# Building the routing's first twelve columns of comparisons during the last attention heads instead of after them

## The chip, the cores and the metric

One core of one Trainium2 chip runs the whole program. The metric is device time in microseconds (us), from start to end of one execution. The kernel is a single launch of three parts that follow each other: an attention, a mixture-of-experts layer whose routing depends on the attention's result, and a second feed-forward layer over the routed rows.

The engines are named as the profile names them. PE is TensorE (matmuls and transposes), DVE is VectorE, ACT is ScalarE, POOL is GpSimd, and SP is the queue that issues most transfers. Each engine works through its own list of instructions in the order in which the program wrote them.

## The reference

```
def _attn_ref(q, k, v, g_q, g_k):                  # 4 batches, 12 heads, 448 tokens, head dim 64
    q_n, k_n = (rmsnorm(q, g_q), rmsnorm(k, g_k))
    scores = scale * np.matmul(q_n, k_n.transpose(0, 1, 3, 2))
    scores = scores - np.max(scores, axis=-1, keepdims=True)
    attn = np.exp(scores)
    attn = attn / (np.sum(attn, axis=-1, keepdims=True) + 1e-09)
    return np.matmul(attn, v)

def _moe_ref(x, w_gate, w1, w2):                   # 1792 tokens, width 768, 8 experts, hidden 1024
    cap = N // E                                   # 224 tokens for each expert
    logits = x @ w_gate
    order = np.argsort(-logits.flatten())          # all token-expert pairs, best first
    for idx in order:                              # a token goes to its best expert that has room
        tok, e = (int(idx) // E, int(idx) % E)
        if assigned[tok] >= 0 or counts[e] >= cap:
            continue
        assigned[tok] = e
        counts[e] += 1
    for e in range(E):
        h = np.maximum(x[assigned == e] @ w1[e], 0.0)
        out[assigned == e] = h @ w2[e]
    return out

def _moe2_ref(x, w_in, w_out):                     # hidden 2048
    h = x @ w_in
    g = h * (1.0 / (1.0 + np.exp(-1.702 * h)))
    return g @ w_out
```

All tensors are float32. The order in which pairs are taken decides which tokens an expert gets, so the kernel has to rank tokens by their logits exactly.

## The kernel before

**Attention.** 48 heads follow each other (4 batches of 12, numbered 0 to 47). The list `ORDER` writes out, for each head, the order in which pieces of work are put on the engines' lists. The names that matter here: K0 and K1 are the score matmuls of the two halves of the head (tile `S`, two buffers), M0 and M1 the row maxima on DVE (line 233), E0 and E1 the exponentials on ACT, A0 to A3 the transposes on PE (tile `pA`, two buffers) of the head before, C0 to C3 the copies of those transposes (on ACT or DVE by `COPY_ENGINE`; block 1 is always on DVE), TQ and TK the transposes of the next head's queries and keys, LK the low part of the keys on DVE (`klo`, line 214), AV the product with the values. At odd heads XT transposes a finished pair of heads back to tokens and XP scales it on DVE (`xt`, line 305). GA and GB give the gate's logits of a batch. S4 and S5 are places where other work is let in, by a call of `slot(h, 4)` or `slot(h, 5)`. TQ, TK, XT, GA, GB and the routing's rows all use one PSUM buffer, the tile `tp`; who writes it next waits until its last reader is done.

**Conversion.** `Convert` turns the second layer's weights from 64-bit words into floats, 48 pieces of two steps each: 512 KB in, two ACT operations (`wab`, `wc`), two DVE operations (`wc`, lines 900 and 905), 256 KB out. One step is let in at S4 of every head up to 45; the rest runs beside the first experts, paced by a budget in `Moe.back`.

**Routing.** The tokens lie as 16 columns of 112; batch b fills columns 4b to 4b+3. `choose` finds each token's best expert and logit (six short DVE operations, lines 538 to 543). `row` spreads the logits of four columns over all partitions (four transposes into `tp`, one ACT copy into `vr`). `compare(j, t0, t1)` builds, on DVE, the 0/1 tile of the tokens of columns t0 to t1 against column j (lines 772 and 774: strictly less up to column j, less or equal behind it). `rank` gathers four such tiles and multiplies them with `Cp` on PE, so that PSUM counts for each token how many better ones each expert has. `same(j)` adds the tie mask of the diagonal on POOL (lines 759 and 760). `last_columns` does `choose`, `row` and `rest` for columns 12 to 15 once the last batch's logits are there; `rest` builds the tiles of columns 13, 14 and 15 on ACT by a Sign and a Relu of 112x1344 each (lines 554 and 555), and four diagonals on POOL. `close` then picks the expert that fills first and the ids of its tokens, and only then the first expert's weights and rows can be fetched.

`Route.first` is a generator: each `next(early)` runs it to its next `yield`. Before the change it is called at S5 of heads 44 to 47 (`choose` for columns 0 to 11, then the three rows), twice between the transposes of head 47, and the rest in `beside` after the attention. The counts go into the four banks of `S`, which are free only once the last exponentials of head 47 have read their scores; the tiles go into buffers of the attention that are free by then (`A`, `AT`).

In `Attn.run` the three calls at the end read

```
        beside(BESIDE[0])
        s.gate_b(s.B - 1, 1)
        beside(0)
...
        beside(BESIDE[1])
```

and `beside(0)` stands for `last_columns`.

Of the kernel before, what the change touches and what calls it, by code (L numbers as in the profile page):

```python
# [20 lines left out]
FT = mybir.dt.float32  # L21
FR = mybir.dt.float32r
F16 = mybir.dt.float16
# [3 lines left out]
OP = mybir.AluOpType  # L27
# [2 lines left out]


SLOT_CONVERT = ((4,), (4,))
BESIDE = [3, 5, [(48, 1), (48, 3)]]
LO_VECTOR = [(0, 2, 4, 6, 8, 10, 12), (1, 3, 5, 7, 8, 11, 13)]
IDLE = (2, 4, 5)
GATE_A = (0, 4)
# [15 lines left out]
class Attn:  # L52
# [294 lines left out]
    def wide(s):  # L347
        return s.ps.tile([128, 4, 112], FT, name="tp", bufs=1)[:112]
# [15 lines left out]
    def buffer2(s):  # L364
        t = s.io.tile([112, 4, 256], FT, name="qt", bufs=3).rearrange("p a b -> p (a b)")
        return t.bitcast(F16)[:, 0:1344].rearrange("p (j t) -> p j t", t=112)

    def small(s):
        return s.ps.tile([128, 4, 112], FT, name="pA", bufs=2)


    def run(s, slot, beside):
# [86 lines left out]
        s.gate_a(s.B - 1, 1)  # L459
# [3 lines that stand above are left out]
        for pr in (last - 2, last - 1, last):  # L463
            s.xtok(pr, True)
            s.put_x(pr, True)
        beside(BESIDE[1])


class Route:
# [241 lines left out]
    def phase(s, k):  # L711
# [28 lines left out]
        if k in (1, 3):  # L740
            yield from s.together(n, n - 4, small)

    def first(s, rank, wide, small, buffer, buffer2):

        nc, V, wk = s.nc, s.nc.vector, s.wk
        s.tiles()
        s.choose(0, 12)
        yield
        for c in range(3):
            s.row(c, wide())  # L750
            yield
        bank = rank()

        ready, diag = {}, {}

        def same(j):
            e = wk.tile([112, 112], FT, name="Be", bufs=1)
            d = wk.tile([112, 112], F16, name="Bd", bufs=16)
            nc.gpsimd.tensor_scalar(e, s.vr[:, j], s.v[:, j:j + 1], None, op0=OP.is_equal)
            nc.gpsimd.tensor_tensor(d, e, s.before, op=OP.mult)  # L760
            diag[j] = d

        def compare(j, t0, t1):
            sv = s.v[:, j:j + 1]
            b = ready.pop((j, t0), None)
            onact = b is not None
            if not onact:
                b = buffer(t0)
            d = diag[j] if t0 <= j < t1 else None
            k = min(max(j + 1, t0), t1)  # L770
            if t0 < k and not onact:
                V.tensor_scalar(b[:, 0:k - t0], s.vr[:, t0:k], sv, None, op0=OP.is_lt)
            if k < t1:
                V.tensor_scalar(b[:, k - t0:t1 - t0], s.vr[:, k:t1], sv, None, op0=OP.is_le)

            s.rank(j, b, d, bank, t0, t1, j < 4, j >= 12)

        def rest():
            for i in ON_ACT[0]:
                b = buffer2()  # L780
                s.lower(b[:, 0:12], s.vr[:, 0:12], s.v[:, i:i + 1])
                ready[i, 0] = b
            for i in range(12, 16):
                same(i)

        s.rest = rest
        for j in range(12):
            if j == 0:
                for i in range(12):
                    same(i)  # L790
            compare(j, 0, 12)
            yield
        for j in range(12, 16):
            if j not in ON_ACT[0]:
                compare(j, 0, 12)
        for j in range(12):
            compare(j, 12, 16)
        for j in ON_ACT[0]:
            compare(j, 0, 12)
        s.flush()  # L800
        yield
        for c in range(3):
            nc.scalar.copy(s.ct[:, 4 * c:4 * c + 4], bank[c])
        for j in range(12, 16):
            compare(j, 12, 16)
        s.flush()
        cnt = wide()
        s.counts(0, 12, cnt)
        nc.scalar.copy(s.ct[:, 12:16], bank[3])
        s.counts(12, 16, cnt)  # L810
        for _ in s.close(0, 16, small):
            pass
# [428 lines left out]
def kernel(  # L1241
# [31 lines left out]
    with ExitStack() as actx:  # L1273
        attn = Attn(actx, tc, q, k, v, g_q, g_k, w_gate, dict(identf=identf, identr=identr), xd, rec[:, :, 0:8])
        attn.ident128 = ident128
        route = Route(tc, consts, wk, rec, identf, ident128, dram)
        early = route.first(attn.rank_banks, attn.wide, attn.small, attn.buffer, attn.buffer2)

        def slot(h, at):
            if 0 <= h < 46:  # L1280
                for _ in range(SLOT_CONVERT[h % 2].count(at)):
                    conv.step()
            if at == 5 and h in (44, 45, 46, 47) or (h, at) in BESIDE[2]:
                next(early)

        def beside(n):
            if n:
                for _ in range(n):
                    next(early)
            else:  # L1290
                route.last_columns(attn.wide)

        attn.run(slot, beside)
        for _ in early:
            pass
# [35 lines left out]
```

## Time and profile before

| what | value |
|---|---|
| median of 3 runs | 1256.66 us (1256.13 to 1257.18) |
| the profiled execution | 1258.07 us, of which the span from first to last instruction is 1256.2 us |
| PE busy | 1147.1 us (91% of the span) |
| DVE busy | 854.4 us (68%) |
| ACT busy | 659.2 us (52%) |
| POOL busy | 703.8 us (56%) |
| granted PE clock, mean | 0.952 of full speed |

The busy shares are means over stages that differ. The stretch that the change touches lies between 293 us (head 43) and 365 us (the first expert's rows are gathered), 6% of the span. A chain of waits lists, in order of time, the pieces of work that each had to wait for the one ahead. The times of the tables below count from the start of the span.

### The profile page before, as it was taken

How to read it: one execution, taken by the hardware profiler on the slowest of the kernel's cores; microseconds unless marked ns; L12 is line 12 of the kernel's file. 1: busy time of each engine (PE TensorE's matmuls, PEld its weight loads, DVE VectorE, ACT ScalarE, POOL GpSimd, SP SyncE). 2: the span in 40 equal slices, each digit the busy share in tenths (PEclk: the TensorE clock that was granted, in tenths of full speed). 3: DMA queues.
4: the chain of work that ended last, by engine and by line, in shares of the span. 5: the costliest groups of instructions: out<-in, count | busy, mean ns of one | idle time of the engine just before them, and what ended most of it. 6: DMA issues, size and time to landing. Idle time of an engine off the chain costs nothing.

```text
span 1256.2 us, 19391 instructions
## 1 busy us (share of the span) xinstructions
PE 1147.1 (91%) x6952; PEld 965.6 (77%) x6952; DVE 854.4 (68%) x1525; ACT 659.2 (52%) x1289; POOL 703.8 (56%) x591
## 2 busy tenths in 40 slices
PE   4899999999858978789999999999999899999995
PEld 3677677766436867679889898998889799889995
DVE  7799999998779879687677836538864535751100
ACT  4798898888622356653335554224544323545420
POOL 3688688873634546455634765546454455445552
PEclk9799999999958889889999999999999899999998
DMA  6454555432043399944346634337633245753421
GB/s 164 118 136 130 150 130 141 127 97 67 24 120 109 98 265 277 276 149 160 117 130 174 183 115 116 121 98 208 192 110 117 93 120 151 199 166 113 135 78 33
DMA packets 185504, 172.95 MB, mean 138 GB/s; under 512 B 9536, under 2 KB 159808, under 8 KB 185408
## 3 DMA queue, kind: packets, MB, share of 16 engines
q1 hardware_dynamic: 180080, 160.55, 45.3%
q0 software_dynamic: 4224, 11.14, 2.9%
q8 instruction: 55, 0.90, 0.3%
q14 instruction: 41, 0.34, 0.1%
q10 hardware_dynamic: 1104, 0.03, 0.0%
HBM read 147.96 MB, written 23.72 MB: 137 GB/s over the span
## 4 chain that ended last, share of the span: by engine, by line
PE 67%; DVE 19%; DMA 5%; issue 5%; ACT 2%; POOL 1%; SPq 0%; POOLq 0%; DVEq 0%; ACTq 0%
PE mm L1029 12%; PE mm L1031 12%; PE mm L1030 12%; PE S L222 6%; PE mm L1040 5%; PE av L269 5%; PE pA L249 5%; PE mm L1041 3%; DMA dout<-wc 2%; DVE gs L1086 2%; DVE wc L900 2%; DVE B L571 2%; DVE tt L1082 2%; DMA xg<-xd,idx 1%; DVE B L569 1%
## 5 line engine op out<-in xcount | busy, mean ns | idle before, releaser
L968 POOL TENSOR_TENSOR wlo<-raw,whi 128x768 fp32r<-128x768 f32 (+1 forms) x175 | 382.3, 2187 | 384.0 <-ACT whi L965 361.3
L965 ACT CAST whi<-raw 128x768 fp32r<-128x768 f32 (+1 forms) x224 | 207.0, 924 | 151.5 <-issue 61.5
L1029 PE MATMUL mm<-gs,whi 128*128 128x448 f32 (+1 forms) x432 | 159.6, 369 | 0.5 <-DVE zs L1079 0.5
L1031 PE MATMUL mm<-gs,wlo 128*128 128x448 f32 (+1 forms) x432 | 156.2, 361 | 0.0
L1030 PE MATMUL mm<-gs,whi 128*128 128x448 f32 (+1 forms) x432 | 156.1, 361 | 0.0
L1031 PE MATMUL mm<-zs,wlo 128*128 128x448 f32 x384 | 143.3, 373 | 7.1 <-POOL wlo L968 4.0
L1029 PE MATMUL mm<-zs,whi 128*128 128x448 f32 x384 | 144.8, 377 | 3.1 <-ACT whi L965 3.1
L1030 PE MATMUL mm<-zs,whi 128*128 128x448 f32 x384 | 142.7, 372 | 1.4 <-DVE zs L1088 1.4
L240 ACT ACTIVATE A<-S,sm 112x448 f32<-112x448 f32 x192 | 122.6, 658 | 6.5 <-DVE sm L233 6.5
L1040 PE MATMUL mm<-gs,whi 128*128 128x448 f32 x336 | 111.6, 387 | 14.6 <-DVE gs L1086 12.7
L233 DVE TENSOR_REDUCE sm<-S 112x2 f32<-112x896 f32 x96 | 104.1, 1085 | 21.3 <-PE S L222 20.1
L1040 PE MATMUL mm<-xs,whi 128*128 128x448 f32 x336 | 111.6, 389 | 0.5 <-ACT whi L965 0.4
L249 PE MATMUL pA<-ident,A 112*112 112x112 f32 x768 | 100.9, 266 | 2.6 <-DVE AT L258 2.4
L1101 DVE TENSOR_TENSOR gs<-sg,gs 128x448 fp32r<-128x448 f32 x64 | 42.2, 662 | 82.5 <-ACT gs L1100 82.4
L249 PEld LDWEIGHTS pA<-ident,A 112*112 112x112 f32 x768 | 85.1, 137 | 14.9 <-DVE AT L258 3.6
L1029 PEld LDWEIGHTS mm<-gs,whi 128*128 128x128 f32 x432 | 83.6, 193 | 10.6 <-issue 4.3
L1099 ACT ACTIVATE sg<-mm 128x448 f32<-128x448 f32 x64 | 34.9, 545 | 104.6 <-PE mm L1031 104.6
L1031 PEld LDWEIGHTS mm<-gs,wlo 128*128 128x128 f32 x432 | 83.5, 193 | 6.1
L1030 PEld LDWEIGHTS mm<-gs,whi 128*128 128x128 f32 x432 | 83.7, 194 | 5.7
L1041 PE MATMUL mm<-xs,wlo 128*128 128x224 f32 x336 | 83.1, 275 | 3.6 <-POOL spacer L1138 1.9
L1031 PEld LDWEIGHTS mm<-zs,wlo 128*128 128x128 f32 x384 | 73.8, 192 | 15.1 <-POOL wlo L968 5.2
L1041 PE MATMUL mm<-gs,wlo 128*128 128x224 f32 x336 | 84.3, 272 | 1.0 <-DVE wlo L968 1.0
(229 smaller groups left out, 2626.1 us busy)
## 6 DMA issues: line engine op xcount, KB each, us to landing
raw<-in_moe_w_dram SPq DMA_DIRECT2D x64, 384.0 KB, 3.5
raw<-in_moe_w_dram SPq DMA_DIRECT2D x48, 512.0 KB, 5.1
raw<-din SPq DMA_DIRECT2D x64, 384.0 KB, 3.1
raw<-dout SPq DMA_DIRECT2D x48, 512.0 KB, 3.7
r<-in_moe_w_in_dram SPq DMA_DIRECT2D x24, 512.0 KB, 4.4
r<-in_moe_w_out_dram SPq DMA_DIRECT2D x24, 512.0 KB, 5.0
din<-wc SPq DMA_DIRECT2D x24, 256.0 KB, 4.2
dout<-wc SPq DMA_DIRECT2D x48, 128.0 KB, 4.9
```

What stands on the lines that cost most here:

```text
L222: nc.tensor.matmul(p[:, c, 0:448], s.qT[h][:, i, :], mv.rearrange("p i t -> p (i t)"), start=(n == 0), stop=(n == 1))
L233: s.nc.vector.tensor_reduce(s.sums[h][:, 2 * u:2 * u + 2, 0], s.Sp[u][:, :, 0:448], axis=AX.X, op=OP.max, negate=True)
L240: s.nc.scalar.activation(s.A[h][:, i, :], p[:, c, 0:448], AF.Exp, bias=sm[:, i, 0:1], scale=1.0, accum_out=sm[:, i, 1:2])
L249: nc.tensor.transpose(p[:, qc], s.A[h][:, qc, kc * 112:(kc + 1) * 112], s.identf)
L269: nc.tensor.matmul(p[hh * 64:(hh + 1) * 64, :], s.grp[g]["v"][:, hl, kc * 64:(kc + 1) * 64], s.AT[h][:, kc, :], start=(kc == 0), stop=(kc ...
L965: nc.scalar.copy(hi, t)
L968: f = lambda: eng.tensor_tensor(lo, t, hi.bitcast(FT), op=OP.subtract)
L1029: nc.tensor.matmul(p, hi[:, k], x[0], start=first, stop=False)
L1030: nc.tensor.matmul(p, hi[:, k], x[1], start=False, stop=False)
L1031: nc.tensor.matmul(p, lo[:, k], x[0], start=False, stop=last)
L1040: a = lambda: nc.tensor.matmul(p, hi[:, k], x.rearrange("p h t -> p (h t)"), start=first, stop=last)
L1041: b = lambda: nc.tensor.matmul(p[:, 0:224], lo[:, k], x[:, 0], start=False, stop=False)
```

## The change

The routing of columns 0 to 11 starts earlier and is cut in two. `choose` is called at S5 of head 42, the three rows at S4 and S5 of head 43 and at S4 of head 44. From S5 of head 44 on, twelve new steps build the twelve comparison tiles of columns 0 to 11 on DVE and keep them in `ready`, in buffers that a new function `buffer3` takes (`kt`, `qt`, `qp`, `kd`, `sq`, `sk`). The banks of `S` are asked for afterwards, at the end of head 47, and three further steps put the counting matmuls of these tiles on PE, four columns at a time. A table `EARLY` says at which place how many steps are run. The conversion's steps at heads 44 and 45 are dropped from there, so that these two steps are run later.

```
-BESIDE = [3, 5, [(48, 1), (48, 3)]]
+BESIDE = [1, 0]
+EARLY = [(42, 5), (43, 4), (43, 5), (44, 4), (44, 5), (45, 4), (45, 4), (45, 5), (46, 4), (46, 4), (46, 5),
+         (47, 4), (47, 4), (47, 5), (48, 0), (48, 0), (48, 1), (48, 3)]
...
+    def buffer3(s, j):
+
+        k = (j - 1) % 3
+        if j == 0:
+            s.room = s.io.tile([112, 4, 256], FT, name="kt", bufs=3).rearrange("p a b -> p (a b)")
+        elif j < 4:
+            s.room = s.io.tile([112, 4, 256], FT, name="qt", bufs=3).rearrange("p a b -> p (a b)")
+        elif j < 10:
...
+            s.room = s.wide_room[:, k * 672:k * 672 + 672]
+        else:
+            s.room = s.wk.tile([112, 16, 64], FT, name="sq" if j == 10 else "sk", bufs=1).rearrange("p a b -> p (a b)")
+        return s.room[:, 0:672].bitcast(F16).rearrange("p (j t) -> p j t", t=112)
...
         for c in range(3):
             s.row(c, wide())
             yield
-        bank = rank()
-
...
-            if k < t1:
+            if k < t1 and not onact:
                 V.tensor_scalar(b[:, k - t0:t1 - t0], s.vr[:, k:t1], sv, None, op0=OP.is_le)
...
         for j in range(12):
+            b, sv = buffer3(j), s.v[:, j:j + 1]
+            V.tensor_scalar(b[:, 0:j + 1], s.vr[:, 0:j + 1], sv, None, op0=OP.is_lt)
+            if j < 11:
+                V.tensor_scalar(b[:, j + 1:12], s.vr[:, j + 1:12], sv, None, op0=OP.is_le)
+            ready[j, 0] = b
             if j == 0:
                 for i in range(12):
                     same(i)
+            yield
+        for j in range(12):
+            if j == 0:
+                bank = rank()
             compare(j, 0, 12)
-            yield
+            if j % 4 == 3:
+                s.flush()
+                yield
...
         def slot(h, at):
-            if 0 <= h < 46:
+            if 0 <= h < 44:
                 for _ in range(SLOT_CONVERT[h % 2].count(at)):
                     conv.step()
-            if at == 5 and h in (44, 45, 46, 47) or (h, at) in BESIDE[2]:
+            for _ in range(EARLY.count((h, at))):
                 next(early)
```

`BESIDE[1]` is now 0, and the three calls at the end of `Attn.run` are as they were, so the last of them calls `last_columns` a second time.

Where the instructions stand, on PE first: the rows of the routing among the transposes into `tp` (`v` is a column's logits, `xu` a finished pair of heads). Before, at the end of head 45:

```order
L269 MATMUL av<-AT,vt 64x448 x4
L293 MATMUL tp<-ident_62,xu 112x128 x4
L549 MATMUL tp<-ident_62,v 112x112 x4
L222 MATMUL S<-khi,qT 112x448
L222 MATMUL S<-klo,qT 112x448
```

With the change, at the end of head 43:

```order
L271 MATMUL av<-AT,vt 64x448 x4
L568 MATMUL tp<-ident_62,v 112x112 x4
L295 MATMUL tp<-ident_62,xu 112x128 x4
L568 MATMUL tp<-ident_62,v 112x112 x4
L224 MATMUL S<-khi,qT 112x448
L224 MATMUL S<-klo,qT 112x448
```

Two rows now stand around the pair's transposes, ahead of the next head's scores, where one stood; the third row moves from the end of head 47 to head 44.

On ACT, the end of the attention (`vr` is the row of columns 12 to 15, `qt` a Sign or Relu of `rest`, `kt` the last three pairs of heads, `ct` the finished counts). Before:

```order
L550 COPY vr<-tp 112x448
L554 ACTIVATE qt<-vr,v 112x1344
L555 ACTIVATE qt<-qt 112x1344
L554 ACTIVATE qt<-vr,v 112x1344
L555 ACTIVATE qt<-qt 112x1344
L554 ACTIVATE qt<-vr,v 112x1344
L555 ACTIVATE qt<-qt 112x1344
L301 COPY kt<-pA 112x512 x2
L301 COPY kt<-av 112x512
L803 CAST ct<-S 128x448 x3
```

With the change, from the third Relu on:

```order
L574 ACTIVATE qt<-qt 112x1344
L303 COPY kt<-pA 112x512 x2
L303 COPY kt<-av 112x512
L569 COPY vr<-tp 112x448
L573 ACTIVATE qt<-vr,v 112x1344
L574 ACTIVATE qt<-qt 112x1344
L573 ACTIVATE qt<-vr,v 112x1344
L574 ACTIVATE qt<-qt 112x1344
L573 ACTIVATE qt<-vr,v 112x1344
L574 ACTIVATE qt<-qt 112x1344
L831 CAST ct<-S 128x448 x3
```

The row's copy and its six activations stand on ACT's list twice, the second time between the pairs' copies and the counts.

On DVE, the end of the attention, from the last batch's logits (`rec`) on, with the change:

```order
L341 TENSOR_REDUCE rec_68<-prod 112x4x8
L557 TENSOR_REDUCE v<-rec_68 112x4
L558 TENSOR_TENSOR ra_3849<-rec_68,v 112x32
...
L562 TENSOR_TENSOR Cp<-ra_3849,alive 112x4x8
L557 TENSOR_REDUCE v<-rec_68 112x4
...
L562 TENSOR_TENSOR Cp<-ra_3849,alive 112x4x8
L789 TENSOR_SCALAR A<-vr,v 112x1344
L791 TENSOR_SCALAR vt<-vr,v 112x448 x12
```

`choose` stands there twice, and behind it one comparison of columns 0 to 11 (column 12) where there were fifteen instructions for columns 5 to 12; the twelve `vt` are the comparisons with the tokens of columns 12 to 15.

## Rows read from the trace of the kernel before

**Rows 1.** Chain of waits, end of the attention: start (us), length, work and count.

```profile
334.50 0.45 PE tp L329 x4
...
353.90 1.41 ACT ct L803 x3
```

**Rows 2.** Heads 45, 46, 47, the counting: length, busy time by engine, PE clock, DMA.

```profile
305.00:312.70 7.70, 6.92 (x51) 4.85 (x49) 6.87 (x16) 6.37 (x17) 0.00 (x0) 1.00 0.14 42
312.70:318.75 6.05, 6.05 (x48) 4.42 (x45) 4.21 (x7) 5.10 (x15) 3.98 (x8) 1.00 0.46 125
318.75:325.90 7.15, 7.15 (x47) 4.21 (x45) 3.48 (x6) 5.01 (x14) 4.71 (x10) 1.00 0.01 2
...
338.30:354.00 15.70, 10.38 (x73) 3.22 (x73) 15.70 (x32) 8.78 (x10) 10.81 (x11) 0.71 0.18 45
```

**Rows 3.** Chain of waits at heads 43 and 45: start (us), length, work and count.

```profile
294.17 0.88 DVE rec L339
295.06 1.00 DVE sm L233
...
296.64 0.59 PE pA L249 x4
...
298.89 0.58 PE tp L293 x4
...
311.56 0.70 DVE xt L305
312.31 0.59 PE tp L549 x4
```

**Rows 4.** Timeline of ACT: start (us), length, work, and idle time before it.

```profile
299.55 0.68 ACT L886 ACTIVATE wab<-r 128x512 f32<-128x512 f32 x1
300.11 0.69 ACT L887 ACTIVATE wc<-r 128x512 int32<-128x512 uint32 x1
...
337.09 0.54 ACT L550 COPY vr<-tp 112x448 f32<-112x448 f32 x1 [2.65 <-PE tp L549]
...
342.87 1.40 ACT L554 ACTIVATE qt<-vr,v 112x1344 f16<-112x1344 f32 x1
...
345.53 1.05 ACT L301 COPY kt<-pA 112x512 f32<-112x512 f32 x2
346.47 0.60 ACT L301 COPY kt<-av 112x512 f32<-112x512 f32 x1
```

**Rows 5.** Timeline of DVE: start (us), length, work.

```profile
305.45 0.20 DVE L538 TENSOR_REDUCE v<-rec 112x12 f32<-112x96 f32 x1
...
307.03 1.08 DVE L233 TENSOR_REDUCE sm<-S 112x2 f32<-112x896 f32 x1
...
345.56 6.97 DVE L774 TENSOR_SCALAR vt<-vr,v 112x448 f16<-112x448 f32 x12
...
353.93 0.44 DVE L772 TENSOR_SCALAR vt<-vr,v 112x448 f16<-112x448 f32 x1
```

**Rows 6.** Busy time of the comparisons of columns 0 to 11, line 772, then line 774.

```profile
327.40:344.60 17.20, 7.30 (x12) 1.00 0.00 1
...
327.40:345.50 18.10, 6.88 (x11) 0.98 0.00 1
```

**Rows 7.** Counting matmuls of four columns: durations (ns, least, median, most), first and last start.

```profile
L592 PE MATMUL S<-A,Cp x12: 352/353/363, 338.3 to 338.7; 112*32 112x448 f16 x12
```

**Rows 8.** Stretches around one PE gap (columns as Rows 2).

```profile
503.00:505.00 2.00, 0.38 (x2) 0.36 (x3) 0.33 (x1) 1.44 (x3) 1.84 (x3) 1.00 0.98 233
505.00:507.00 2.00, 2.00 (x8) 1.76 (x7) 1.59 (x3) 0.68 (x1) 1.18 (x1) 0.56 1.05 375
507.00:509.00 2.00, 2.00 (x8) 1.79 (x7) 0.66 (x1) 1.36 (x3) 0.00 (x0) 0.58 1.06 369
```

**Rows 9.** The stretch of the conversion's last eleven pieces (columns as Rows 2).

```profile
497.00:541.00 44.00, 33.75 (x141) 28.40 (x140) 30.60 (x54) 27.63 (x47) 19.25 (x12) 0.87 0.92 277
```

**Rows 10.** The conversion's first ACT operation there: durations, first and last start.

```profile
L886 ACT ACTIVATE wab<-r x11: 658/672/703, 496.9 to 531.9; 128x512 f32<-128x512 f32 x11
```

More of the change, by code (lines that the diff above doesn't have):

```diff
@@ L366, in buffer2 @@
         return t.bitcast(F16)[:, 0:1344].rearrange("p (j t) -> p j t", t=112)
+    def buffer3(s, j):
[5 more added lines that the diff above has]
+        elif j < 10:
+            if k == 0:
+                s.wide_room = (s.wk.tile([112, 16, 128], FR, name="qp").bitcast(FT) if j < 7 else
+                               s.wk.tile([112, 16, 2, 64], FT, name="kd").rearrange("p a b c -> p a (b c)"))
+                s.wide_room = s.wide_room.rearrange("p a b -> p (a b)")
+            s.room = s.wide_room[:, k * 672:k * 672 + 672]
+        else:
+            s.room = s.wk.tile([112, 16, 64], FT, name="sq" if j == 10 else "sk", bufs=1).rearrange("p a b -> p (a b)")
+        return s.room[:, 0:672].bitcast(F16).rearrange("p (j t) -> p j t", t=112)
     def small(s):
@@ L741, in phase, with first @@
             yield from s.together(n, n - 4, small)
-    def first(s, rank, wide, small, buffer, buffer2):
+    def first(s, rank, wide, small, buffer, buffer2, buffer3):
         nc, V, wk = s.nc, s.nc.vector, s.wk
@@ L1276 @@
         route = Route(tc, consts, wk, rec, identf, ident128, dram)
-        early = route.first(attn.rank_banks, attn.wide, attn.small, attn.buffer, attn.buffer2)
+        early = route.first(attn.rank_banks, attn.wide, attn.small, attn.buffer, attn.buffer2, attn.buffer3)
         def slot(h, at):
-            if 0 <= h < 46:
+            if 0 <= h < 44:
                 for _ in range(SLOT_CONVERT[h % 2].count(at)):
                     conv.step()
-            if at == 5 and h in (44, 45, 46, 47) or (h, at) in BESIDE[2]:
+            for _ in range(EARLY.count((h, at))):
                 next(early)
```

## The prediction, made before the changed kernel ran

> **What bounds the kernel now.** I read the chain of waits first, then stretches of the timeline head by head. In the heads the chain runs almost wholly on PE, which is busy for all of heads 46 and 47 and for all but 0.8 us of head 45 [rows 2]. The reader should see in the same rows how much of each head VectorE is idle: 0.8, 1.8 and 3.7 us. At the end of head 42 the chain leaves PE: the reduction of the logits, the row maximum of head 43, a copy, and only then the transposes that PE waits for [rows 3]. After the heads it leaves PE again. While the comparisons are counted VectorE is busy for 15.70 of 15.70 us and PE waits for it [rows 2], from the gate's last transposes at 334.50 to the first copy of finished counts at 353.90 [rows 1]. So comparisons on VectorE cost time after the heads, and the heads seem to have room. What the room costs is decided by what else stands in the queues.
>
> **The change part by part.**
>
> *`choose` at the end of head 42.* Its six operations take 1.58 us, from 305.45 to the maximum behind them at 307.03 [rows 5]. They now stand between `rec` and the maximum of head 43, two pieces that follow each other on the chain without a gap, and the transposes at 296.64 wait on what comes behind [rows 3]. All but a tenth lies on the path: +1.5 us. Its old place at head 44 is not on the chain, so nothing comes back. Bounds: 0.5 (PE catches up) to 1.6.
>
> *Rows 0 and 1 at head 43.* Both stand on PE ahead of the scores of head 44, around the pair's transposes, and all three write the one buffer `tp`. Row 0 is copied by ACT, and on ACT's list the two conversion operations of this head's step stand ahead of that copy. They begin at 299.55 and 300.11 and end near 300.7 [rows 4]; with the 1.5 us of `choose` in front, near 302.3. The copy takes 0.5, so the pair's transposes start near 302.8 where they started at 298.89 [rows 3], 3.9 later. Then row 1 waits for the pair's scaling, 0.70 as at 311.56, and itself takes 0.59 [rows 3]. In all the scores of head 44 come 5.3 us late, 3.8 more than `choose` alone makes. Queued behind the waiting transposes is all of PE's work. Bounds: 2.5 (if ACT's exponentials are less late than VectorE) to 4.2.
>
> *Row 2 at head 44.* Only its own 0.4 us on PE.
>
> *The comparisons, heads 44 to 47.* Twelve tiles in 23 instructions have 7.30 + 6.88 = 14.2 us of busy time [rows 6]. Instructions of one engine overlap by 0.08 us in the timeline, so they occupy VectorE for 12.3, or 1.03 a tile. One fits into head 44. For heads 45 to 47 VectorE's list was 6.87 + 4.21 + 3.48 = 14.6 us [rows 2]. It loses `choose` (1.6) and one conversion step (0.6) and gains eleven tiles (11.3): 23.7 us. It also starts a microsecond after the head's first scores. PE's list over these heads was 20.9 us [rows 2], and without the rows and their wait it is near 19. So VectorE is late by head 47, and late then are the copies of the transposes of heads 46 and 47, which hold `pA`. Against before, the last of these transposes come 1 to 2 us later.
>
> *Counting on PE.* Three groups of 12 matmuls and 4 diagonals now stand among the last gate's steps. Twelve start within 0.4 us [rows 7], so a group takes about 0.65, and the first two are in front of the gate's last step. With the point above: lower bound +0.5 (VectorE not late, 1.5 us of row wait at head 45 saved, 2.0 us of groups added), upper +3.0 (the queue of 23.7 us in full). I take +2.3, nearer the upper end, since 23.7 is far above 19.
>
> Up to the row of the last columns that makes 1.5 + 3.8 + 0.4 + 2.3 = **+8.0 us**.
>
> *PE's clock.* At head 43 PE waits some 2.1 us before the pair's transposes and a further 1 us before row 1. The nearest row is the stretch at 503, where PE worked 0.38 of 2 us. There the clock stood at 0.56 and 0.58 of full for the next 4 us [rows 8], mostly the 1.2 GHz level, which cost 4 x 0.43 = 1.7 us. The wait of 0.8 us at head 45 cost nothing: the clock there is 1.00 [rows 2]. I take **+1.7**, with 0 as the lower end. The Trainium skill, "TensorE: Matmul & The Clock Gate", Part 1, says that an idle TensorE is throttled to half its rate and gets the full rate back only after it has been busy again. The trace agrees at 505, and the rule speaks against any wait put on PE. By it alone head 47's wait would cost the same again, 1.7 more.
>
> *`last_columns` twice.* `beside(BESIDE[1])` is now `beside(0)`. The second `choose` overwrites `v`, which the first pass's three Signs on ACT and four diagonals on GpSimd still read, so VectorE stops until the third Sign is done. Behind it are the comparison of column 12 and, after the second row, the twelve `vt`. Count from the start T of the first row's copy, before at 337.09 [rows 4]. The third Sign ended at 344.27, T + 7.2. ACT goes on with its Relu to T + 8.4 (345.53), then the three copies, 1.5 us, to T + 10.0 [rows 4]. Only then comes the second row's copy, and another 8.4 us to the last Relu at T + 18.4. VectorE's `vt`, 6.97 us [rows 5], end at T + 17.5 and are hidden. From the last `vt` (345.56 + 6.97 = 352.53) to the first copy of counts (353.90) were 1.4 us [rows 1, 5]. Counts are therefore copied at T + 19.8, where before it was 353.90 - 337.09 = 16.8: **+3.0 us**. Without the second pass the `vt` would end near T + 8.4 (0.5 for the row, 0.9 for column 12, 6.97), and the counts would be copied at T + 10.0, behind ACT's three copies, which is 6.8 us better than before. That is the most that the change can give here, and the second pass takes it all.
>
> *The conversion.* One piece moves from heads 44 and 45 to the end of the conversion, where eleven pieces [rows 10] go with 44.0 - 33.75 = 10.25 us of idle PE [rows 9]: **+0.9 us** a piece. Bounds: 0, and 4 (a whole 44/11 us of it). The ACT and VectorE time that it leaves in the heads is counted above.
>
> **Sum.** 8.0 + 1.7 + 3.0 + 0.9 = +13.6 us, on the profiled execution's 1258.07: 1271.7. The median of the runs is 1.4 below that execution, so against it I predict **1270.3 us**.
>
> **The rivals.**
> 1. *The clock holds at head 43.* For it: head 45's wait left it at 1.00. Against it: the wait is now more than twice as long. 1270.3 - 1.7 = 1268.6.
> 2. *The heads absorb the early work.* For it: VectorE's idle time above. Against it: the `tp` chain is on PE and ACT, where VectorE's room doesn't help. Up to the row +0.5 instead of 8.0, clock full: 0.5 + 3.0 + 0.9 = +4.4, 1261.1.
> 3. *Faster: the second pass hides.* Place: VectorE's list after the row. Price: -6.8 instead of +3.0. It decides if ACT's second pass ends before VectorE's comparisons and the delay up to the row, clock included, stays under 3.4 us. With that at 0.5: -6.8 + 0.5 + 0.9 = -5.4, 1251.3. Against it: the second row's copy is behind the three copies on ACT by the program's own order.
> 4. *GpSimd slows the comparisons.* GpSimd now makes its twelve diagonals beside the tiles of heads 45 and 46. In the `vt`, of which a part ran beside GpSimd, one took 6.97/12 = 0.58 us, where a like comparison alone took 0.44 less the overlap of 0.08 [rows 5]; at that ratio six tiles (6.2 us) would cost at most 3.8 more, and as most of this is in the mean of 1.03 already, I count +2.5: 1272.8. The Trainium skill, "GPSIMD Engine Reference", Key points, says that GpSimd shares its SBUF interfaces with VectorE and contends with some of its modes.
> 5. *The conversion's end costs its upper bound*, 4 instead of 0.9: 1273.4.
>
> **How the numbers follow.** Chances: the sum as it stands 0.42, rival 1 0.20, rival 2 0.12, rival 3 0.03, rival 4 0.12, rival 5 0.07, no difference that can be told 0.04. The lowest case of the sum without rival 2 is 0.5 + 2.5 + 0.4 + 0.5 + 3.0 = 6.9, 1263.6; the highest is 1.6 + 4.2 + 0.4 + 3.0 + 1.7 + 3.0 + 4 = 17.9, 1274.6, and a part of rival 4 may come on top. The range from 1263 to 1275.5 leaves out rivals 2 and 3 and the far end. A measurement here can tell 0.2%, 2.5 us, from no change. Slower by more 0.93, within 0.04, faster 0.03.
>
> **What the next profile would show.** The maximum of head 43 behind `choose`, its start some 1.5 us later. The pair's transposes of head 43 waiting 2 us for ACT's copy of `vr`, the second row waiting for `xt`, and the granted clock near 0.5 in the 4 us behind. No gap of VectorE in heads 45 to 47, and PE waiting for its copies in head 47. After the attention a gap of 7 us on VectorE that ends with the third Sign, six further activations on ACT, and the counts' copy near T + 20. The gate's last transposes near 344. I am wrong if the scores of head 44 start less than 3 us late, or if VectorE doesn't wait for the third Sign.

## The result and the profile after

The changed kernel takes **1270.48 us**, median of 4 runs (1266.83 to 1273.35), where the kernel before took 1256.92 beside it (1256.13 to 1259.51), 13.6 us less. The ratio of the runs is 1.0114, with a 95% interval of 1.0083 to 1.0144, so it is slower. The profiled execution took 1269.44 us with a span of 1267.6. That is 11.4 more than the span before.

The table divides this by five marks in the timelines: the logits' reduction of the third batch (`rec`, start), the first scores of head 44, the first scores of head 45, the copy of the last columns' row T (`vr`), and the first copy of counts (`ct`). A sixth is the first routing's `eid`.

| stretch, us | before | after | difference | forecast |
|---|---|---|---|---|
| start to `rec` | 294.17 | 291.28 | -2.89 | 0 |
| `rec` to head 44 | 5.06 | 10.92 | +5.86 | +5.3 |
| head 44 to head 45 | 5.72 | 8.48 | +2.76 | +2.1 |
| head 45 to T | 32.14 | 34.31 | +2.17 | +2.3 |
| T to `ct` | 16.81 | 19.39 | +2.58 | +3.0 |
| `ct` to `eid` | 6.44 | 6.44 | 0.00 | 0 |
| `eid` to the end | 895.9 | 896.8 | +0.9 | +0.9 |

Up to `rec` the two kernels do the same work. The 2.89 us there are a matter of the execution (see the table of runs below).

Timeline of PE, after the change, those lines with a wait in front of them, and the first scores of head 44 (last bracket: idle time before, and what ended it):

```profile
295.48 0.60 PE L251 MATMUL pA<-ident,A 112*112 112x112 f32 x4 [1.75 <-DVE AT L260]
300.09 0.65 PE L295 MATMUL tp<-ident,xu 128*112 128x128 f32 x4 [1.84 <-ACT vr L569]
301.52 0.99 PE L568 MATMUL tp<-ident,v 112*112 112x112 f32 x4 [0.79 <-DVE xt L307]
302.20 0.69 PE L224 MATMUL S<-khi,qT 128*112 128x448 f32 x1
...
328.12 0.60 PE L251 MATMUL pA<-ident,A 112*112 112x112 f32 x4 [1.60 <-DVE AT L260]
...
352.49 0.99 PE L568 MATMUL tp<-ident,v 112*112 112x112 f32 x4 [5.16 <-DVE v L557]
```

The first three waits, 4.4 us together, stand where [rows 3] had the chain through `rec`, maximum and transposes: PE waits for what comes behind `choose`, then for ACT's copy of row 0, then for the pair's scaling ahead of row 1. The wait of 1.60 at 328.12, in head 47, is for VectorE. At 352.49 PE waits for the second pass's `v`.

Stretches of the same execution: head 43 and 44, then heads 45, 46 and 47, then the counting (columns as in [rows 2]):

```profile
299.28:301.28 2.00, 0.65 (x4) 0.41 (x4) 0.50 (x1) 0.76 (x2) 1.00 (x2) 0.84 0.27 51
301.28:303.28 2.00, 1.75 (x7) 1.62 (x8) 0.19 (x1) 0.53 (x1) 1.69 (x4) 0.50 0.79 260
303.28:305.28 2.00, 2.00 (x11) 1.77 (x10) 1.09 (x1) 0.48 (x1) 1.72 (x4) 0.50 0.24 66
305.28:307.28 2.00, 2.00 (x10) 1.71 (x9) 0.62 (x1) 1.28 (x5) 1.64 (x5) 0.50 0.00 0
307.28:309.28 2.00, 2.00 (x17) 1.49 (x17) 1.60 (x2) 1.44 (x4) 1.74 (x4) 0.95 0.00 0
...
310.70:316.80 6.10, 6.10 (x48) 4.48 (x45) 5.29 (x8) 5.36 (x14) 4.53 (x8) 1.00 0.00 0
316.80:323.50 6.70, 6.19 (x44) 4.13 (x41) 6.70 (x12) 3.96 (x12) 0.50 (x1) 1.00 0.14 37
323.50:330.20 6.70, 5.09 (x34) 3.49 (x34) 6.67 (x14) 4.36 (x14) 0.00 (x0) 1.00 0.00 0
...
345.90:364.40 18.50, 9.03 (x35) 3.29 (x34) 10.80 (x26) 17.31 (x17) 12.02 (x19) 0.50 0.15 37
```

Behind the waits the clock stands at 0.50, the 1.2 GHz level, for 6 us, through the scores of head 44. In heads 46 and 47 PE and VectorE have changed places against [rows 2]: VectorE is busy for 6.70 of 6.70 and 6.67 of 6.70 us, PE for 6.19 and 5.09. In the counting VectorE is no longer full (10.80 of 18.50), and ACT nearly is (17.31).

Timeline of ACT, end of the attention:

```profile
344.99 0.53 ACT L569 COPY vr<-tp 112x448 f32<-112x448 f32 x1 [2.65 <-PE tp L568]
...
350.76 1.40 ACT L573 ACTIVATE qt<-vr,v 112x1344 f16<-112x1344 f32 x1
...
354.36 0.60 ACT L303 COPY kt<-av 112x512 f32<-112x512 f32 x1
354.83 0.56 ACT L569 COPY vr<-tp 112x448 f32<-112x448 f32 x1
...
362.06 1.32 ACT L574 ACTIVATE qt<-qt 112x1344 f16<-112x1344 f16 x1
364.38 1.40 ACT L831 CAST ct<-S 128x448 f16<-128x448 f32 x3 [1.00 <-PE S L611]
```

Timeline of VectorE, the same place:

```profile
352.24 0.19 DVE L557 TENSOR_REDUCE v<-rec 112x4 f32<-112x32 f32 x1 [6.88 <-ACT qt L573]
...
355.42 6.82 DVE L791 TENSOR_SCALAR vt<-vr,v 112x448 f16<-112x448 f32 x12 [1.03 <-ACT vr L569]
```

VectorE stops for 6.88 us until the third Sign (350.76 + 1.40 = 352.16) has read `v`. The second row's copy follows the pairs' copies on ACT. Against [rows 4], where ACT was done with the copies 6.8 us before `ct`, it now works through to 363.38.

### The profile page after: what moved, and what is told of

It reads as the page before. It is cut to its first block, busy times and chain, and to the rows that moved or that the text cites. A ratio compares the mean times of both kernels' runs of the same rounds, so it can differ in the third digit from the quotient of the medians.

```text
span 1267.6 us, 19426 instructions
## 1 busy us (share of the span) xinstructions
PE 1147.6 (91%) x6956; PEld 966.2 (76%) x6956; DVE 848.4 (67%) x1531; ACT 667.5 (53%) x1296; POOL 704.0 (56%) x599
## 4 chain that ended last, share of the span: by engine, by line
PE 45%; DVE 9%; issue 4%; DMA 3%; POOL 2%; ACT 1%; SPq 0%; POOLq 0%; DVEq 0%; ACTq 0%
PE mm L1057 12%; PE mm L1059 11%; PE mm L1058 11%; PE mm L1068 5%; PE mm L1069 3%; DVE gs L1114 2%; DVE tt L1110 1%; POOL wlo L996 1%; DMA dout<-wc 1%; PE tr L1150 1%; DVE O L662 1%; DMA xg<-xd,idx 1%; DVE B L588 1%; PE tr L1047 1%; DVE wlo L996 1%
## 5 line engine op out<-in xcount | busy, mean ns | idle before, releaser
L224 PE MATMUL S<-khi,qT 128*112 128x448 f32 x192 | 80.9, 421 | 5.5 <-ACT khi L212 5.5
```

Source lines behind the costliest of these rows:

```text
L224: nc.tensor.matmul(p[:, c, 0:448], s.qT[h][:, i, :], mv.rearrange("p i t -> p (i t)"), start=(n == 0), stop=(n == 1))
```

## The experiments

Each was timed in turn with the kernel before. The table has the profiled execution of each by the marks, and the recorded ratio of its runs to those of the kernel before, with its 95% interval (the quotient of the two medians differs from it by up to 0.2%). The column from `rec` to `eid` holds everything that the change touches except the conversion. The edits of `e1`, `e3`, `e4`, `e7` and `e8` are shown against the changed kernel, those of `e2`, `e6`, `e9` and `e10` against the kernel before.

| run | start to `rec` | `rec` to head 44 | head 44 to 45 | `rec` to T | T to `ct` | `rec` to `eid` | `eid` to end | ratio |
|---|---|---|---|---|---|---|---|---|
| before | 294.17 | 5.06 | 5.72 | 42.92 | 16.81 | 66.17 | 895.9 | 1 |
| after | 291.28 | 10.92 | 8.48 | 53.71 | 19.39 | 79.54 | 896.8 | 1.0114 [1.0083, 1.0144] |
| e1_once | 291.28 | 11.38 | 8.26 | 54.01 | 9.85 | 70.32 | 895.6 | 1.0065 [1.0042, 1.0087] |
| e2_before_twice | 294.21 | 5.05 | 5.73 | 42.95 | 20.40 | 69.79 | 903.9 | 1.0046 [1.0027, 1.0065] |
| e3_rows_apart | 294.11 | 8.19 | 7.28 | 51.17 | 9.85 | 67.48 | 895.0 | 1.0017 [1.0002, 1.0031] |
| e4_convert_kept | 290.89 | 11.04 | 6.08 | 52.13 | 9.85 | 68.43 | 893.6 | 1.0086 [1.0066, 1.0107] |
| e5_changed_again | 294.36 | 10.83 | 7.46 | 52.6 | 19.39 | 78.44 | 895.0 | 1.0121 [1.0098, 1.0144] |
| e6_rows_only | 291.06 | 11.04 | 6.07 | 47.08 | 16.39 | 69.24 | 897.8 | 1.0078 [1.0062, 1.0095] |
| e7_choose_later | 293.44 | 7.79 | 7.29 | 50.79 | 9.85 | 67.09 | 901.9 | 1.0016 [1.0, 1.0033] |
| e8_row_by_row | 294.58 | 5.05 | 5.73 | 43.62 | 10.36 | 62.19 | 893.4 | 0.9962 [0.994, 0.9985] |
| e9_choose_only | 293.02 | 7.79 | 6.31 | 46.08 | 16.94 | 68.79 | 899.7 | 1.0021 [0.9992, 1.005] |
| e10_rows_again | 293.31 | 10.92 | 7.09 | 47.70 | 16.79 | 70.26 | 900.1 | 1.0053 [1.003, 1.0076] |

**The second pass of `last_columns`.** The theory is the prediction's: the pass costs 3 us by itself, and 9.8 of what the change could have given. The rival is that it hides behind the other engines.

`e1_once`: the changed kernel with one pass.

```diff
-        beside(BESIDE[1])
```

> The changed kernel with the last call in the attention's end taken out, so that the last columns are chosen, spread and compared once; the output is the reference's. Theory (the second pass sets the end of the counting): the counts are copied 10.0 us after the last row instead of 19.8, so 9.8 us less than the changed kernel: 1270.5 - 9.8 = 1260.7 us. Rival (the second pass hides behind VectorE's comparisons, and the lateness of the heads is the whole loss): within 2 us of 1270.5. Second rival (only ACT's second set of six activations, 8 us, of which VectorE's list hides 5): 1267.5.

`e2_before_twice`: the kernel before, with a second pass.

```diff
+        beside(0)
```

> The kernel before with the second pass over the last columns added and nothing else changed; the output is the reference's. Theory: ACT's list (three activations pairs, three copies, row, three pairs again) sets the end as in the changed kernel, so the counts are copied 19.8 us behind the last row instead of 16.8: 1256.9 + 3.0 = 1259.9 us. Rival (VectorE's comparisons, which here still stand behind the last row, hide it): 1256.9 within 0.5. Other side (VectorE's stop for the third Sign adds to its own list, since five tiles stand behind the second choose): 1263 or more.

With one pass the first copy of counts starts 9.85 us after T instead of 19.39, and `rec` to `eid` is 9.2 us shorter. Timeline of ACT in `e1_once`:

```profile
345.29 0.53 ACT L568 COPY vr<-tp 112x448 f32<-112x448 f32 x1 [2.71 <-PE tp L567]
...
354.66 0.60 ACT L303 COPY kt<-av 112x512 f32<-112x512 f32 x1
355.14 1.42 ACT L830 CAST ct<-S 128x448 f16<-128x448 f32 x3
```

The counts' copy follows the pairs' copies without a wait: what ends last is now ACT's list. In `e2_before_twice` the second pass alone costs 3.6 us up to `ct` and up to `eid`. It doesn't hide in either kernel.

**Head 43.** The theory: `choose` and the rows around one pair's transposes cost 1.5 and 3.8 us, and the wait lowers the clock. Rivals: PE's wait is caught up by heads 44 to 47, or the comparisons' queue on VectorE is what costs.

`e3_rows_apart`: one pass, and row 0 behind the pair's transposes of head 43, the other two rows in head 44.

```diff
-EARLY = [(42, 5), (43, 4), (43, 5), (44, 4), (44, 5), (45, 4), (45, 4), (45, 5), (46, 4), (46, 4), (46, 5),
+EARLY = [(42, 5), (43, 5), (44, 4), (44, 5), (44, 5), (45, 4), (45, 4), (45, 5), (46, 4), (46, 4), (46, 5),
...
-        beside(BESIDE[1])
```

> As e1_once, with the three rows of columns 0 to 11 moved: row 0 from ahead of the pair's transposes of head 43 to behind them, row 1 from there to head 44, row 2 one place later in head 44. Theory (the chain through the one buffer at head 43 and the clock behind it cost some 5.5 us of which the wait for ACT's copy goes): 3 us less than e1_once, 1257.6 us, and no granted clock under 0.9 in head 44. Rival (VectorE's list of comparisons sets the heads' lateness, so a stall ahead of it is made good): no difference from e1_once within 1 us.

Head 44 starts 3.2 us earlier than in `e1_once`, and T comes 2.8 us earlier. The clock is 1.00 in every stretch of heads 43 and 44, with the wait of 1.78 for `choose` still there (in the first line):

```profile
296.11:298.11 2.00, 0.44 (x5) 0.23 (x3) 1.93 (x5) 0.28 (x1) 0.00 (x0) 1.00 0.00 0
298.11:300.11 2.00, 1.79 (x12) 0.86 (x12) 2.00 (x4) 2.00 (x7) 0.00 (x0) 1.00 0.00 0
300.11:302.11 2.00, 1.22 (x10) 0.58 (x7) 1.60 (x3) 2.00 (x7) 0.00 (x0) 1.00 0.03 8
```

In `e1_once` the clock stood at 0.50 from 297 to 307 us, so the 3.2 and the 2.8 hold the clock as well as the rows. `e4_convert_kept` (below) has the rows around the transposes and the full clock in head 44. Against it head 44 starts 2.85 us earlier here, but T comes only 0.96 earlier. The rows around one pair's transposes are thus a real cost at head 44. Most of what moving them saves is lost again by T: rows 1 and 2 make head 44 longer (7.28 against 6.08), and VectorE holds up the heads behind. Stretches of heads 45 to 47 in this run:

```profile
309.60:315.70 6.10, 6.10 (x48) 4.48 (x45) 5.29 (x8) 4.93 (x13) 5.29 (x10) 1.00 0.00 0
315.70:322.60 6.90, 6.17 (x43) 4.12 (x40) 6.90 (x12) 3.93 (x11) 4.39 (x7) 1.00 0.14 36
322.60:329.40 6.80, 5.21 (x32) 3.57 (x32) 6.77 (x14) 4.46 (x14) 0.00 (x0) 0.91 0.00 0
```

VectorE has no room in heads 46 and 47. From head 45 to T the run takes 35.70 us, the changed kernel 34.31.

`e6_rows_only`, and the same once more as `e10_rows_again`: the kernel before, with `choose` and the three rows at their new places and nothing else changed.

```diff
-            if at == 5 and h in (44, 45, 46, 47) or (h, at) in BESIDE[2]:
+            if (h, at) in ((42, 5), (43, 4), (43, 5), (44, 4)) or (h, at) in BESIDE[2]:
```

> The kernel before with only the first choice and the three rows of columns 0 to 11 moved to the changed kernel's places (heads 42 to 44); comparisons, counting, conversion and a single pass over the last columns as before. The output is the reference's. Theory (the early rows cost the lateness of head 44, and heads 45 to 47 give back the 2.3 us that the rows cost there): the last row's copy comes 3.3 us later against the third batch's logits, 5.7 where the clock falls; the counts 16.8 us behind it as before: 3.3 to 5.7 us more than the kernel before. Rival (VectorE's comparisons cause the lateness, a stall of PE in head 43 is made good in the heads after it): no difference within 1 us.

> The run with choose and the rows alone moved, once more, for a second profile. Open is why its runs have a median 9 us above the kernel before, where the parts of its profiled execution add up to 3. Theory: TensorE's clock falls in head 43 or 44 in most executions and did not in the profiled one. Then this profile has the scores of heads 44 and 45 more than 7 us apart (6.07 in the first one) and the counts' copy 2 us later behind the last batch's logits than 63.5. Rival: the clock holds again (6.1 us), the counts' copy again at 63.5, and the runs again have a median of 1263 to 1266; then the difference does not come from the heads, and the stretch in front of the logits' reduction or behind the routing has to show it, with times outside of 291 to 294 us and 893 to 904 us.

`e9_choose_only`: the kernel before, with `choose` alone at the end of head 42.

```diff
-            if at == 5 and h in (44, 45, 46, 47) or (h, at) in BESIDE[2]:
+            if at == 5 and h in (42, 45, 46, 47) or (h, at) in BESIDE[2]:
```

> The kernel before with one thing changed: choose for the first twelve columns stands at the end of head 42, between the logits' reduction and the row maximum of head 43, instead of head 44. By the prediction's first term its 1.58 us lie on the path: PE waits about 1.75 us before the transposes of head 43 (as in the changed kernel, 1.75), the scores of head 44 start 1.5 us later (6.6 us behind the last batch's logits, before 5.06) and nothing comes back: the row of the last columns is copied at 44.4 behind the logits (before 42.9), the time is +1.5 us. The rival reads the runs with choose moved by a head, where the scores of head 44 moved by 0.4 only: PE catches up in head 43, or the place at head 44 was on the path too, and the row comes at 42.9 to 43.3, the time +0 to +0.4. By both the clock stands at its full level in heads 43 and 44: the scores of heads 44 and 45 begin 5.7 to 6.1 us apart.

Head 44 is as late in both runs of the rows alone (11.04 and 10.92) as in the changed kernel (10.92), so the delay comes from these two moves and not from the comparisons. From head 45 to T the rows alone save 2.2 us (29.97 against 32.14), and with the comparisons it is 35.01 in `e4_convert_kept`, which keeps the conversion's step as the rows alone do, and 34.31 in the changed kernel, which doesn't: the twelve tiles and the groups cost 4.3 to 5.0 us in front of T. With `choose` alone head 44 is 2.7 us late and T 3.2, where 1.5 and the full clock were expected. Of the 2.7 the wait is 1.75, and the rest is the clock, by the line of this wait and the stretches of this run:

```profile
297.22 0.59 PE L249 MATMUL pA<-ident,A 112*112 112x112 f32 x4 [1.75 <-DVE AT L258]
...
297.02:299.02 2.00, 1.80 (x10) 0.86 (x12) 2.00 (x4) 2.00 (x7) 0.00 (x0) 0.92 0.00 0
299.02:301.02 2.00, 2.00 (x9) 0.97 (x6) 0.89 (x2) 2.00 (x6) 0.00 (x0) 0.50 0.04 8
301.02:303.02 2.00, 2.00 (x14) 1.72 (x13) 1.21 (x2) 0.48 (x2) 0.00 (x0) 0.73 0.35 49
```

Where the clock falls differs between executions of the same program. Stretches of `e6_rows_only` and a line of its PE, then stretches of `e10_rows_again`; PE's wait for ACT's `vr` stands in the fourth stretch of the first, in the first stretch of the second:

```profile
293.06:295.06 2.00, 0.42 (x5) 0.21 (x3) 1.93 (x5) 0.28 (x1) 0.00 (x0) 1.00 0.00 0
295.06:297.06 2.00, 1.78 (x9) 0.82 (x10) 2.00 (x4) 2.00 (x7) 0.00 (x0) 0.77 0.00 0
297.06:299.06 2.00, 2.00 (x8) 0.60 (x5) 0.91 (x2) 2.00 (x7) 0.00 (x0) 0.50 0.04 8
299.06:301.06 2.00, 1.28 (x8) 0.68 (x6) 0.07 (x1) 0.89 (x2) 0.62 (x2) 0.88 0.31 51
301.06:303.06 2.00, 1.32 (x9) 1.16 (x10) 0.63 (x1) 0.54 (x1) 1.72 (x4) 1.00 0.74 248
...
300.31 0.65 PE L293 MATMUL tp<-ident,xu 128*112 128x128 f32 x4 [0.62 <-ACT vr L550]
```

```profile
301.31:303.31 2.00, 0.65 (x4) 0.41 (x4) 0.50 (x1) 0.76 (x2) 1.00 (x2) 0.93 0.31 39
303.31:305.31 2.00, 1.75 (x7) 1.61 (x8) 0.20 (x1) 0.53 (x1) 1.68 (x4) 0.50 0.76 270
305.31:307.31 2.00, 2.00 (x15) 1.76 (x15) 1.23 (x2) 0.53 (x1) 1.72 (x4) 0.72 0.25 68
```

In `e6_rows_only` it falls right behind the wait for `choose`. PE's slow work then lies mostly in the time in which it would have waited for `vr`: that wait is 0.62 instead of 1.84, and the pair's transposes start 9.25 us behind `rec` instead of 8.81. Head 44 runs at full speed: 6.07 us. In `e10_rows_again` it falls behind the second wait, and head 44 takes 7.09; in the changed kernel 8.48, in its second profile 7.46. So the fall costs head 44 nothing, 1.0, 1.4 or 2.4 us, by where it comes.

The theory put on record for `e10_rows_again`, that the clock falls in most executions and did not in the first profile, holds in part: it fell there too, but in front of a wait. The heads' scores are 7.09 us apart as expected, the counts' copy came 1.0 us later behind `rec` instead of 2. This execution is 4.1 us longer than the kernel before from `rec` to `eid`, and 4.2 behind `eid`, and its runs are 6.7 us longer (ratio 1.0053). The heads explain some 4 of it. The 4.2 behind `eid`, like `e9_choose_only`'s 3.8, lie in a stretch that takes 893 to 904 us in these executions of the same later work. Whether the change has a part in it stays open.

`e7_choose_later`: as `e3_rows_apart`, with `choose` a head later.

```diff
-EARLY = [(42, 5), (43, 4), (43, 5), (44, 4), (44, 5), (45, 4), (45, 4), (45, 5), (46, 4), (46, 4), (46, 5),
+EARLY = [(43, 4), (43, 5), (44, 4), (44, 5), (44, 5), (45, 4), (45, 4), (45, 5), (46, 4), (46, 4), (46, 5),
...
-        beside(BESIDE[1])
```

> As e3_rows_apart (last columns once, rows at head 43's end and in head 44), with the first choice moved from the end of head 42 to head 43, ahead of the pair's scaling. Theory (the six operations of the choice lie on the chain at the end of head 42 and are hidden in head 43): the scores of head 44 start 1.5 us earlier against the third batch's logits than in e3_rows_apart (8.2 us), so 6.7 us; but if VectorE's list of comparisons sets the end of the heads, the last row's copy (51.2 us behind those logits in e3_rows_apart) comes less than 0.5 us earlier. Rival: PE waits for the choice at row 0 instead, and nothing is gained at head 44 either.

Head 44 starts 0.4 us earlier than in `e3_rows_apart`, and T comes 0.4 earlier. PE's wait of 1.78 is gone, but `choose` now stands ahead of the pair's scaling, and PE waits there for `xt`: 2.15 us, where it was 0.78.

```profile
300.87 0.59 PE L567 MATMUL tp<-ident,v 112*112 112x112 f32 x4 [2.15 <-DVE xt L307]
```

This place in head 43 isn't free either.

**The conversion.** `e4_convert_kept`: one pass, and the conversion's step of heads 44 and 45 at its old place.

```diff
-        beside(BESIDE[1])
...
-            if 0 <= h < 44:
+            if 0 <= h < 46:
```

> As e1_once, with the conversion's steps at heads 44 and 45 kept. Theory: one piece less at the conversion's end (0.9 us saved), one more VectorE operation in head 45 (0.6 us lost): 0.3 us less than e1_once, 1260.4 us. Rival (a piece at the conversion's end costs its whole period): 3 us less, 1257.7. Other side (the ACT operations of the step stand ahead of the row's copy in head 44 or the comparisons are later): 1 us more.

The profile and the runs contradict each other: its span is 1252.9 (4.3 below `e1_once`), the median of its runs 1264.33 (3.9 above). The marks give a better answer. The conversion's last pieces lie between the second and the third `eid`. This stretch took 160.7, 160.7, 162.8, 160.9 and 165.1 us in the five profiles with the step moved, and 154.1, 161.4, 158.7, 156.2, 158.0, 160.5 and 155.3 in the seven without: 4.3 more in the mean. The stretch behind it took 70.1, 70.1, 68.2, 68.1 and 68.1 against 72.9 to 73.0: 4.0 less. From the first `eid` to the fourth it is 293.6 with the step moved and 293.9 without (means of five and seven values between 290.7 and 298.7). The piece costs nothing that can be told; with values that scatter over 8 us a cost of 0.9 couldn't be seen either.

**The kernel as changed, once more.**

`e5_changed_again` has the changed kernel as it is.

> The changed kernel itself once more, unaltered, beside the next three, so that they and it stand against one kernel before on one chip. Theory: the counts are copied 19.4 us behind the last row's copy again, the scores of head 44 start 5.9 us later against the logits of the third batch; the clock in head 44 need not fall in every execution (head 44 lasts 8.5 us where it falls, 6.1 where it doesn't), so the span's parts can differ by 2.4 us there. 12 to 15 us more than the kernel before.

The ratio is 1.0121 (6 runs, median 1270.46). From `rec` to `eid` it is 1.1 us shorter than the first profile, all of it in head 44 and in its start (18.29 against 19.40 to head 45).

**Profile and runs.** For `e2_before_twice`, `e3_rows_apart` and the runs from `e7_choose_later` to `e10_rows_again` the difference from `rec` to `eid` lies in the interval of the ratio (`e10_rows_again`: 4.1 in 3.8 to 9.6), and for `e5_changed_again` at its lower end (12.27 and 12.3). For three it doesn't: `e1_once` 4.2 (5.3 to 10.9 by the runs), `e4_convert_kept` 2.3 (8.3 to 13.4), `e6_rows_only` 3.1 (7.8 to 11.9). The profiled executions of all three lie under the median of their kernels, by 1.4, 9.5 and 5.3 us; those of `e4_convert_kept` and `e6_rows_only` are the shortest of six. Up to `rec` the three were 3 us short, and in `e4_convert_kept` and `e6_rows_only`, whose head 44 ran at the full clock, a later fall would add up to 2.4. The mean granted clock of `e6_rows_only` was 0.958 in the profiled execution and 0.943 to 0.949 in the other five, so those spent more time at the lower level; in `e4_convert_kept` it was 0.953, and 0.950 to 0.953 in the others. Where the other executions spend their time was not seen, since only one of each has a trace.

**A version for the free time.** `e8_row_by_row`: the rows, `choose` and the conversion at their places of before, one pass, and each tile compared in three parts of four columns, as each row arrives. The first four buffers are three `kt` and a `vt` instead of one `kt` and three `qt`, and all counting matmuls stand behind the last row.

```diff
-BESIDE = [1, 0]
-EARLY = [(42, 5), (43, 4), (43, 5), (44, 4), (44, 5), (45, 4), (45, 4), (45, 5), (46, 4), (46, 4), (46, 5),
-         (47, 4), (47, 4), (47, 5), (48, 0), (48, 0), (48, 1), (48, 3)]
+BESIDE = [14, 10]
+EARLY = [(44, 5), (45, 5)] + 5 * [(46, 5)] + 9 * [(47, 5)] + 3 * [(48, 1)]
...
+        def cell(j, c):
...
+            b, sv = ready[j, 0], s.v[:, j:j + 1]
+            t0, t1 = 4 * c, 4 * c + 4
...
+        for c in range(3):
+            s.row(c, wide())
             yield
+            for j in ((), range(4), range(4, 12))[c]:
+                cell(j, 0)
+                yield
+        for c in (1, 2):
+            for j in range(12):
+                cell(j, c)
+                yield
```

> A version that keeps the early building of comparisons but leaves the choice, the rows and the conversion where they were before: each row of four columns is compared as soon as it has been copied, 4 tiles' parts in head 46, 8 in head 47, 17 while PE does the last products, 7 behind the last row; counting behind the last row; one pass over the last columns. Theory (VectorE's idle time at the ends of heads 46 and 47 and during the last products hides 29 of 36 parts, and nothing is put in PE's way): the last row's copy within 0.5 us of the kernel before, the counts 12.4 us behind it instead of 16.8: 4.4 us less than the kernel before. Rival (comparisons in the heads delay the copies of the transposes, as in the changed kernel): the last row 2 us or more later, at most 2 us less than the kernel before.

It takes 1251.79 us (median of 12 runs) beside 1256.04, ratio 0.9962 [0.994, 0.9985]: the one version that is faster than both. Head 44 starts at 5.05, T comes 0.7 us later than before (within 0.5 was expected), the first counts 10.36 us after T (12.4 was expected). The last comparisons run to T + 3.6 beside the Signs on ACT, whose copies end at T + 10 in any case. Behind `rec` the first counts come 5.75 us earlier than before, and `eid` 4.0 earlier. Timelines of ACT, VectorE and GpSimd there:

```profile
347.28 3.48 POOL L306 TENSOR_TENSOR kt<-kt,rinv 112x512 f32<-112x512 f32 x3 [1.96 <-ACT kt L302]
...
348.56 1.40 ACT L841 CAST ct<-S 128x448 f16<-128x448 f32 x3 [0.39 <-PE S L610]
...
348.65 1.20 DVE L787 TENSOR_SCALAR vt<-vr,v 112x336 f16<-112x336 f32 x1
349.77 1.12 DVE L785 TENSOR_SCALAR vt<-vr,v 112x224 f16<-112x224 f32 x1
...
351.05 0.38 DVE L785 TENSOR_SCALAR vt<-vr,v 112x336 f16<-112x336 f32 x1
...
352.56 0.53 ACT L847 CAST ct<-S 128x448 f16<-128x448 f32 x1 [2.60 <-PE S L616]
```

The last copy of counts still waits 2.60 us: three small comparisons took over a microsecond each beside GpSimd's multiplications, and the same shape 0.38 when these had ended. This part of the gain is not taken yet.

## Why the prediction was right, and where not

The forecast of 1270.3 and the measured 1270.48 agree. That they do so to 0.2 us is luck, since the runs lie between 1266.83 and 1273.35. The steps agree too, with one exception and a few sizes.

- **`choose` and the `tp` chain at head 43**: +5.3 forecast to the scores of head 44, +5.86 measured (5.77 in the second profile). The three waits are the ones named, 1.75, 1.84 and 0.79. `e9_choose_only` shows the first part alone: 1.75 of wait, where the sum had 1.5. About 0.3 and 0.2 of the +5.86 and +5.77 are the lower clock under row 1's transposes: 0.68 and 0.58 us pass from their start to the scores, 0.36 in `e6_rows_only` at the full clock.
- **Rival 2** (the heads absorb the early work) is refuted: VectorE's idle time doesn't shorten waits on PE and ACT. With `choose` alone moved, nothing that can be told comes back by T (3.3 us late at head 45, 3.2 at T).
- **Row 2**: +0.4. Head 44 takes 6.07 and 6.08 with the row and a full clock, 5.72 without: +0.35.
- **Comparisons of heads 45 to 47, and counting**: +2.3, measured +2.17 in both profiles of the changed kernel: the rows gone give -2.2 (`e6_rows_only`), the tiles and groups +4.3. VectorE is the limit of heads 46 and 47, as the queue of 23.7 us said. In head 45 it still has a gap (busy 5.29 of 6.10 us), which the forecast had ruled out.
- **PE's clock**: +1.7, measured 2.4 and 1.4 in head 44. The row at 503 [rows 8] gave the right mechanism and nearly the right size. The Trainium skill, "TensorE: Matmul & The Clock Gate", Part 1, says that an idle TensorE falls to half its rate. The trace agrees at 301.28 (0.50), but `e3_rows_apart` has a wait of 1.78 with the clock at 1.00 throughout, so the rule, put this shortly, doesn't say that a wait here will be paid for. Head 47's wait of 1.60 left the clock at 1.00 (323.50), and the 1.7 that the rule alone would have added there did not come. Rival 1 (the clock holds) didn't occur in either profile of the changed kernel. In `e6_rows_only` the fall was hidden but for 0.4 us, which comes to nearly the same.
- **`last_columns` twice**: +3.0, measured +2.58 in the changed kernel, +3.6 in the kernel before. The count at T + 10.0 without the second pass came at T + 9.85. Rival 3 is refuted: the pass is on the path, and its 9.5 us take more than the 7.0 that the early comparisons gave behind T (16.81 - 9.85).
- **The conversion's piece** is the exception: no run shows its +0.9. The term assumed that the idle PE in front of the conversion's end grows by one piece's share. The runs show 4.3 us more in that stretch and 4.0 less in the next. Over the three stretches from the first `eid` to the fourth the means differ by -0.3, with single values 8 us apart: the 4 us of rival 5 are not seen, and 0.9 can't be told from nothing. The +0.9 behind `eid` in the table is the scatter of 893 to 904 and no confirmation.
- **GpSimd beside the comparisons** (rival 4) didn't come about. Eight of GpSimd's twelve diagonals were done ahead of the first comparison (310.2). The others stood beside four of the 23 comparisons, up to 317.3, and the comparisons were busy for 13.4 us, less than the 14.2 of [rows 6].

For the profiled execution the sum gave 1271.7, and it took 1269.4. Without the conversion it would have been 1270.8. The parts that the change touches came to +13.4 (79.54 - 66.17), against 12.7 forecast for them, and the first 294 us, which it doesn't touch, were 2.9 shorter in this execution.

## What to carry to other kernels

Idle time of an engine is not yet a place for work: ask what stands behind the new piece in its queue, and on which buffer its neighbours wait. In front of T the twelve comparisons cost 4.3 to 5.0 us as whole tiles behind early rows. In `e8_row_by_row`, where they are cut in parts that start when each row comes and no row is moved, T is 0.7 us late and a few parts are left behind it. Which of these differences counts most was not separated. A step that runs twice because a list of steps was edited shows as a second set of the same lines on every engine, and here it took all that the early comparisons gave behind T.

## What the chip showed beside this

- A wait of PE of 1.75 to 1.80 us in the same place was followed by the lower clock at once (`e1_once`, `e4_convert_kept`, `e6_rows_only`, `e9_choose_only`), behind a second wait (`e10_rows_again`, the changed kernel), or not at all (`e3_rows_apart`). Work at the lower clock in front of a further wait cost 0.4 us in `e6_rows_only`.
- Up to `rec`, where all kernels do the same, executions took 290.9 to 294.6 us.
- A comparison of 112x336 took 1.20 us beside GpSimd's multiplication and 0.38 alone. The Trainium skill, "GPSIMD Engine Reference", Key points, says that the two share SBUF interfaces and that GpSimd contends with VectorE instructions in some modes. The trace agrees here. Beside the comparisons of heads 45 and 46 it was GpSimd's diagonals that took longer, 1.15 and 0.79 us where their like took 0.56 and 0.42.
